# Seven block products in place of eight for half of the batches of a three-layer kernel

## The chip, the cores and the metric

The kernel runs on one core of a Trainium2 chip. Its engines work side by side, each through its own list of instructions in order: TensorE (PE) multiplies matrices into PSUM, VectorE (DVE), ScalarE (ACT) and GpSimd (POOL) work on elements, and SyncE (SP) issues all of the kernel's transfers. GpSimd does not touch PSUM here. They wait for each other by semaphores. The metric is the device time of one execution in microseconds.

## The reference

Four batches of 12 heads go through sigmoid attention; the result, 1792 rows of 768, goes through a gated layer and then through a second one:

```python
scores = scale * np.matmul(q, k.transpose(0, 1, 3, 2)) - np.log(S)
attn_out = np.matmul(1.0 / (1.0 + np.exp(-scores)), v)      # 4 x 12 x 448 x 64
x = attn_out.transpose(0, 2, 1, 3).reshape(B * S, H * D)    # 1792 x 768
xn = x / np.sqrt(np.mean(x * x, axis=-1, keepdims=True) + 1e-06) * rms_g
g = xn @ w_gate                                             # 768 x 1536
x = (g / (1.0 + np.exp(-g)) * (xn @ w_val)) @ w_out         # 1536 x 768
h = x @ w_in                                                # 768 x 2048, "w_in2" below
x = (h - np.tanh(h)) @ w_out2                               # 2048 x 768
```

The weights come as 64-bit floats: each arrives as two 32-bit words and is made a 32-bit float on the chip.

## The kernel before

Activations lie with features on the 128 partitions and the 448 rows of one batch along the free side. All matrices are cut into 128 x 128 blocks; KM = 6, KF1 = 12 and KF2 = 16 blocks make 768, 1536 and 2048. Every operand is split into a high part that TensorE takes exactly and a low rest (`h`, `l`), so one block product is three matmuls of 448 columns, hh, hl and lh, summed in PSUM (`block` in `job_units`, L708 to L715).

**Jobs.** The layers are a list of jobs of six weight blocks (NB = 6): phases Ag (w_gate), Av (w_val), B (w_out), C (w_in2), D (w_out2). A job of Ag, Av or C is one column block m of the weights with all six k; a job of B or D holds blocks of a group of four k (GR = 4) for one or two m, and its sums over the groups are added up in `acc` tiles. Batches 0 and 1 go through all layers together, then batches 2 and 3 (the loop at L297); only the first three m of w_gate and w_val are done for batch 0 and batch 1 apart (`ALONE`). A job for two batches is 36 matmuls. The second half of the list, 68 jobs, is for batches 2 and 3; the attention of these batches runs beside the first half.

**Weights.** For each job `load` brings 768 KB of raw words into one of two `raw` tiles; `conv` makes 32-bit floats of it in a `cv` tile (two of them): `fields` (L365 on ScalarE, L368, L372 or L371, L374), `join` (L378), then `high` (a cast, L274) and `low_part` (a subtraction, L391) into a `whl` tile. Loads are issued four jobs ahead, conversions are made two jobs ahead (`AHEAD`). The second half loads and converts all weights again.

**Ends.** `epilogue` takes a PSUM bank out: sigmoid and two products for the gate, tanh and a difference for w_in2, copy or addition for B and D; `parts` splits the result for the next layer (cast L274, subtraction L649). x of batches 2 and 3 waits in DRAM and comes back near the end of the first half (`reload_x`, `x_chunk`: a product L634, a scaled cast L637, L638).

**Order.** Nothing is issued as written. `add` collects work with the engines that may do it and an assumed time for each; `Plan.issue` goes through it like a clock and places each piece on the engine where it ends first, so the planner chooses between VectorE, ScalarE and GpSimd, and between buffers. TensorE's matmuls of the layers are one stream in the order of the jobs. Many tiles share pools of slots: `unit` (87 tiles of 448 columns), `ps` (the eight PSUM banks). The kernel's own helper `copy` stands at L274, so casts and copies of all kinds have that line.

## Time and profile before

| | us |
|---|---|
| median of 3 runs | 1213.77 |
| the three runs | 1217.71, 1213.77, 1204.66 |
| profiled execution | 1205.45 |
| its span | 1203.7 |

| engine | busy us of the span | share |
|---|---|---|
| TensorE, matmuls | 1171.0 | 97% |
| VectorE | 1011.6 | 84% |
| ScalarE | 558.5 | 46% |
| GpSimd | 213.0 | 18% |

Transfers moved 136.32 MB. The span is what the profiler saw of the profiled execution; 1.75 us of its time lie around it. A matmul's busy time includes its way through the pipeline, so a busy TensorE tells that it did not pause, not how dense its matmuls stand; for that one counts matmuls in a stretch. In rows, L12 is line 12 of the kernel, `out<-in` are the tiles written and read (their numbers left out), x is a count.

### The profile page before, as it was taken

To read this page: it belongs to the slowest core of one execution; us is meant where nothing else is said; L and a number is where in the kernel's file an instruction comes from. 1 tells how busy PE (TensorE), PEld (TensorE's weight loads), DVE (VectorE), ACT (ScalarE), POOL (GpSimd) and SP (SyncE) were. 2 spreads that over 40 slices of the span, in tenths; PEclk is the share of its full clock that TensorE was granted. 3 is DMA by queue.
4 is the path that set the end of the run, shared out by engine and by line. 5 is a ranking of instruction groups with operands and counts; after the bars stand their busy time and mean duration, and the time that the engine had idled before them with its cause. 6 is when DMAs were issued, how large, how long until landed. Compare 5 with 4: busy or idle time off the path is not lost.

```text
span 1203.7 us, 15461 instructions
## 1 busy us (share of the span) xinstructions
PE 1171.0 (97%) x5886; PEld 1027.0 (85%) x5886; DVE 1011.6 (84%) x1429; ACT 558.5 (46%) x858; POOL 213.0 (18%) x131
## 2 busy tenths in 40 slices
...
GB/s 170 191 156 175 67 31 109 135 99 122 106 117 116 68 85 90 117 116 110 113 135 157 98 152 125 111 124 113 105 121 109 62 110 135 121 106 107 110 47 92
DMA packets 41786, 136.32 MB, mean 113 GB/s; under 512 B 7280, under 2 KB 22768, under 8 KB 41712
## 3 DMA queue, kind: packets, MB, share of 16 engines
...
q14 instruction: 28, 0.23, 0.1%
HBM read 127.06 MB, written 8.26 MB: 112 GB/s over the span
## 4 chain that ended last, share of the span: by engine, by line
PE 77%; DVE 12%; ACT 4%; DMA 3%; issue 2%; SPq 1%; POOL 1%; DVEq 0%; ACTq 0%; POOLq 0%
PE ps L712 71%; PE ps L466 3%; DVE raw L374 2%; DVE cv L378 2%; DVE raw L372 1%; PE ps L505 1%; ACT raw L371 1%; DVE unit L649 1%; DMA raw<-in_w_out 1%; DVE cv L368 1%; ACT unit L274 1%; PE ps L559 1%; PE ps L560 1%; SPq L413 1%; DVE unit L274 1%
## 5 line engine op out<-in xcount | busy, mean ns | idle before, releaser
L712 PE MATMUL ps<-unit,whl 128*128 128x448 f32 x4680 | 968.9, 368 | 7.5 <-DVE unit L545 4.5
L712 PEld LDWEIGHTS ps<-unit,whl 128*128 128x128 f32 x4680 | 881.6, 189 | 88.3 <-issue 6.3
L391 POOL TENSOR_TENSOR whl<-cv,whl 128x768 fp32r<-128x768 f32 x84 | 161.2, 1919 | 710.1 <-DVE whl L274 349.1
L365 ACT ACTIVATE cv<-raw 128x768 uint16<-128x768 uint16 x136 | 148.7, 1093 | 195.5 <-POOL whl L391 78.2
L374 DVE TENSOR_SCALAR raw<-raw 128x768 uint16<-128x768 uint16 x136 | 149.1, 1096 | 32.8 <-ACT raw L371 29.7
L378 DVE SCALAR_TENSOR_TENSOR cv<-raw,cv 128x768 uint32<-128x768 uint32 x136 | 139.5, 1026 | 8.3
L649 DVE TENSOR_TENSOR unit<-unit 128x448 fp32r<-128x448 f32 x130 | 100.4, 788 | 20.9 <-ACT unit L274 17.1
L274 ACT CAST unit<-unit 128x448 fp32r<-128x448 f32 (+1 forms) x117 | 64.2, 566 | 105.5 <-DVE unit L662 54.8
L368 DVE TENSOR_SCALAR cv<-raw 128x768 uint16<-128x768 uint16 x136 | 87.7, 645 | 29.5 <-POOL whl L391 25.7
L372 DVE TENSOR_SCALAR raw<-raw 128x768 uint16<-128x768 uint16 x104 | 109.6, 1054 | 3.4
L274 ACT CAST whl<-cv 128x768 fp32r<-128x768 f32 x65 | 54.4, 837 | 110.8 <-PE ps L712 95.3
L676 DVE TENSOR_TENSOR unit<-ps,unit 128x448 f32<-128x448 f32 x120 | 70.1, 618 | 23.2 <-PE ps L712 22.9
L466 PE MATMUL ps<-unit 64*128 64x448 f32 (+1 forms) x576 | 73.6, 388 | 4.7 <-DVE unit L274 2.7
L466 PEld LDWEIGHTS ps<-unit 64*128 64x128 f32 (+1 forms) x576 | 49.1, 176 | 27.6 <-issue 11.3
L545 DVE TENSOR_TENSOR unit<-ps,unit 128x448 fp32r<-128x448 f32 (+1 forms) x96 | 57.6, 619 | 12.4 <-ACT unit L274 10.8
L371 ACT ACTIVATE raw<-raw 128x768 bf16<-128x768 bf16 x32 | 62.0, 1945 | 8.7 <-DVE cv L368 8.6
L666 ACT ACTIVATE unit<-ps 128x448 f32<-128x448 f32 x64 | 31.5, 541 | 63.8 <-PE ps L712 63.8
L476 ACT ACTIVATE ps<-ps 128x448 f32<-128x448 f32 (+1 forms) x96 | 49.4, 533 | 17.7 <-PE ps L466 17.5
L712 PE MATMUL ps<-unit 128*128 128x448 f32 x216 | 51.1, 387 | 0.9 <-ACT unit L476 0.6
L274 DVE CAST unit<-unit 128x448 fp32r<-128x448 f32 (+1 forms) x68 | 35.9, 528 | 16.1 <-DMA unit<-in_qkt 14.4
L712 PEld LDWEIGHTS ps<-unit 128*128 128x128 f32 x216 | 40.6, 194 | 10.1 <-issue 4.2
L476 ACT ACTIVATE unit<-ps 128x448 f32<-128x448 f32 (+1 forms) x96 | 45.7, 542 | 4.1 <-PE ps L466 3.3
...
## 6 DMA issues: line engine op xcount, KB each, us to landing
raw<-in_w_out SPq DMA_DIRECT2D x56, 768.0 KB, 4.3
raw<-in_w_in SPq DMA_DIRECT2D x32, 768.0 KB, 4.3
raw<-in_w_gate SPq DMA_DIRECT2D x24, 768.0 KB, 4.3
raw<-in_w_val SPq DMA_DIRECT2D x24, 768.0 KB, 4.4
...
out<-unit SPq DMA_DIRECT2D x24, 224.0 KB, 2.0
...
```

The lines of the kernel that those rows point to most:

```text
L274: add(engines, lambda e: (nc.scalar.copy if e == "ACT" else nc.vector.tensor_copy)(to(), of()), reads, writes)
L365: add(act(NW), lambda e: nc.scalar.activation(c16(0), low(), AF.Copy, scale=2.0 ** -13, bias=-0.49995), [r["l"]], [c["l"]])
L368: add(dve(NW, fast=True), lambda e: nc.vector.tensor_scalar(out=c16(1), in0=top(), scalar1=0x8000, scalar2=None, op0=ALU.bitwise_and), [r[ ...
L371: add({**dve(NW, fast=True), **act(NW)}, lambda e: nc.scalar.activation(top(BF16), top(BF16), AF.Abs) if e == "ACT" else nc.vector.tensor_ ...
L372: top(BF16), top(BF16), AF.Abs) if e == "ACT" else nc.vector.tensor_scalar(
L374: add(dve(NW, fast=True), lambda e: nc.vector.tensor_scalar(out=top(), in0=top(), scalar1=0x47EF, scalar2=0x3800, op0=ALU.min, op1=ALU.sub ...
L378: add(dve(NW, psum=False), lambda e: nc.vector.scalar_tensor_tensor(out=c.tile, in0=r.tile[:, :, 1], scalar=3, in1=c.tile, op0=ALU.logical ...
L391: add({**dve(wide, psum=False), **pool(wide)}, lambda e, q=q: ENG[e].tensor_sub(ap(q, "l"), f32(q), ap(q, "h").bitcast(F32)), [c["l"], c[" ...
L466: nc.tensor.matmul(ps[i, c].tile[:n, :S], lhsT=f[w].tile[rows, c * P:c * P + n], rhs=f[q].tile[rows, :], start=(w, q) == ("kh", "qh"), sto ...
L476: add(act(S, psum=True), lambda e: nc.scalar.activation(to.tile[at:at + n, :S], ps.tile[:n, :S], AF.Sigmoid, bias=-math.log(S), scale=1.0 ...
L649: add({**pool(S), **dve(S, psum=False)}, lambda e: ENG[e].tensor_sub(c["l"].tile, t.tile, c["h"].tile.bitcast(F32)), [t["t"], kh], [kl])
L712: nc.tensor.matmul(ps.tile[:, :S], lhsT=wt, rhs=a[p].tile, start=first and i == 0, stop=last and i == 2,)
```

## The change

For batches 2 and 3 the layers of w_gate, w_val and w_in2 take two column blocks at a time. The two batches and the two column blocks are rows and columns of a 2 x 2 product of block matrices, the six k being two interleaved sets of three: the left side is A11, A12, A21, A22 (column block m, k set e), the right side B11, B12, B21, B22 (k set e, batch). Seven products of sums take the place of eight: S1 to S4 are sums of left blocks (`sums` in `halves`), T1 to T4 of right blocks (`right_units`), each side is split into high and low afterwards, and the results are put together by seven additions out of PSUM (`plus` in `seven_units`, L849). The w_out and w_out2 layers stay as they were.

Weights of the second half are no longer loaded and converted anew: in the first half each conversion also stores its result in DRAM (`put`: 384 KB from `cv` for w_gate, w_val and w_in2, 768 KB, split already, from the `whl` tile for the others), and `fetch` reads it three jobs ahead (BACK = 3). Raw, split, fetched tiles and the left operands (`op`) share one pool `wt` of 7 slots, where 2 + 4 were; `unit` has 83 slots, not 87. The sums of the left side are in `cv` tiles.

```diff
-N_UNIT, N_MOE, N_RAW, N_WHL = 87, 44, 2, 4
+N_UNIT, N_MOE, N_RAW, N_WT = 83, 44, 2, 7
+N_AGAIN = 3
+BACK = 3
+BATCHES = ((0, 1), (2, 3))
...
-        "raw": (N_RAW, {"raw": N_RAW}),
+        "wt": (N_WT, {"raw": N_RAW, "whl": N_WT - N_RAW, "again": N_AGAIN, "op": N_WT - N_AGAIN}),
...
+    for names, ph, n in (
+        ([(ph, p) for p in range(KF1 // 2) for ph in ("Ag", "Av")], "B", KF1 // GR),
+        ([("C", p) for p in range(KF2 // 2)], "D", KF2 // GR),
+    ):
+        per, at = len(names) // n, 0
+        for g in range(n):
+            to = min((g + 1) * per + 1, len(names))
+            firsts(names[at:to])
+            second(ph, bs, g)
+            at = to
...
+    def fetch(i):
...
+        w = whls[i] = slot("again", wt_p, [P, 2, NW], dt, "wt")
+        add({"SP": (2200, False)}, lambda e: nc.sync.dma_start(out=w.tile if ph in PAIRS else w.tile.bitcast(F32), in_=d.tile),
+            [d[x] for x in "hl"], [w["h"], w["l"]], after=2000)
...
+        def both(to, x, y, sub=True):
+            (o, ok), (a, ak), (b, bk) = of[to], of[x], of[y]
+            add({**dve(NH, psum=False), **pool(NH)}, lambda e: (ENG[e].tensor_sub if sub else ENG[e].tensor_add)(
+                o(), a(), b()), [*ak, *bk], ok)
+
+        def split(*names):
+            t = slot("op", wt_p, [P, 2, 2, NH], F32R, "wt")
+            for n, name in enumerate(names):
...
+                copy({**act(NH), **dve(NH, fast=True)}, hi, a, ak, [t[n, 0]])
+                add({**dve(NH, psum=False), **pool(NH)}, lambda e, a=a, hi=hi, lo=lo: ENG[e].tensor_sub(
+                    lo(), a(), hi().bitcast(F32)), [*ak, t[n, 0]], [t[n, 1]])
...
+            both("S1", "A21", "A22", sub=False)
+            both("S2", "S1", "A11")
+            both("S3", "A11", "A21")
+            both("S4", "A12", "S2")
+
+        return [sums, lambda: split("A11", "S1"), lambda: split("S2", "S3"), lambda: split("A12", "A22"), lambda: split("S4")]
...
+        def put():
+
+            if ph in PAIRS:
+                add({"SP": (1100, False)}, lambda e: nc.sync.dma_start(out=d.tile[:, at % 2], in_=c.tile.bitcast(F32)),
+                    [c["l"], c["h"]], [d["hl"[at % 2]]], after=2000)
+            else:
+                add({"SP": (2200, False)}, lambda e: nc.sync.dma_start(out=d.tile, in_=w.tile.bitcast(F32)),
+                    [w["h"], w["l"]], [d["h"], d["l"]], after=2000)
+
+        if ph in PAIRS:
+            return [fields, lambda: (join(), put()), high, low_part]
+        return [fields, join, high, lambda: (low_part(), put())]
...
+            f["T1"] = right_sum(b12, b11)
+            f["T2"] = right_sum(b22, f["T1"])
+            f["T3"] = right_sum(b22, b12)
+            f["T4"] = right_sum(b21, f["T2"])
...
+    PRODUCTS = {1: ("A11", "B11"), 5: ("S1", "T1"), 6: ("S2", "T2"), 7: ("S3", "T3"),
+                2: ("A12", "B21"), 4: ("A22", "T4"), 3: ("S4", "B22")}
...
+            add(dve(S), lambda e: nc.vector.tensor_add(t.tile, banks[n].tile[:, :S], x.tile), [banks[n]["t"], x["t"]], [t["t"]])
...
+            def run(e):
+                for q, (a, b) in enumerate(("hh", "hl", "lh")):
+                    nc.tensor.matmul(
+                        ps.tile[:, :S], lhsT=part(a), rhs=x[b].tile,
+                        start=i == 0 and q == 0, stop=i == 2 and q == 2)
...
+        if (ph, p) == ("C", 0):
+
+            order = [(n, i) for n in (1, 5, 6, 7) for i in range(2)] + [(n, 2) for n in (1, 5, 6, 7)]
+        else:
+            order = [(n, i) for n in (1, 5, 6, 7) for i in range(3)]
+        order += [(n, i) for n in (2, 4, 3) for i in range(3)]
...
     for j in range(len(jobs)):
+        fetch(j + BACK)
```

How the order moves is shown at three places. First TensorE, from the norm of batch 3 (the four matmuls of 112 x 1) to the end, before:

```order
L712 MATMUL ps<-unit,whl 128x448 x72
L602 MATMUL ps<-ones,unit 112x1 x4
L712 MATMUL ps<-unit,whl 128x448 x18
L612 MATMUL ps<-dg,ones 128x112 x4
L712 MATMUL ps<-unit,whl 128x448 x2682
```

and of the change (L877 are the products, L921 the jobs as before):

```order
L921 MATMUL ps<-unit,wt 128x448 x72
L691 MATMUL ps<-ones,unit 112x1 x4
L921 MATMUL ps<-unit,wt 128x448 x18
L701 MATMUL ps<-dg,ones 128x112 x4
L921 MATMUL ps<-unit,wt 128x448 x234
L877 MATMUL ps<-unit,wt 128x448 x315
L921 MATMUL ps<-unit,wt 128x448 x144
L877 MATMUL ps<-unit,wt 128x448 x252
L921 MATMUL ps<-unit,wt 128x448 x144
L877 MATMUL ps<-unit,wt 128x448 x189
L921 MATMUL ps<-unit,wt 128x448 x144
```

Of the 2682 matmuls in a row 234 end the first half as before; behind them product stretches of 5, 4 and 3 pairs alternate with 144 matmuls of w_out, and behind the rows shown 189, 126, 126 and 63 matmuls of w_in2's products alternate with 144 of w_out2 in the same way.

Second VectorE, early in the gate and value jobs of the second half, before:

```order
L659 TENSOR_TENSOR unit<-ps,unit 128x448 x2
L378 SCALAR_TENSOR_TENSOR cv<-raw,cv 128x768
L274 CAST whl<-cv 128x768
L391 TENSOR_TENSOR whl<-cv,whl 128x768
L368 TENSOR_SCALAR cv<-raw 128x768
L372 TENSOR_SCALAR raw<-raw 128x768
L374 TENSOR_SCALAR raw<-raw 128x768
```

and of the change in the first product stretch:

```order
L849 TENSOR_TENSOR unit<-ps,unit 128x448 x2
L391 TENSOR_TENSOR wt<-cv,wt 128x384
L828 TENSOR_TENSOR unit<-unit 128x448
L381 TENSOR_TENSOR cv<-wt 128x384
L381 TENSOR_TENSOR cv<-wt,cv 128x384
L828 TENSOR_TENSOR unit<-unit 128x448
L276 CAST wt<-cv 128x384
L391 TENSOR_TENSOR wt<-wt 128x384
```

The passes over 768 raw columns are gone; sums (L381) and splits (L276, L391) of left blocks, PSUM additions (L849) and the gate's product in SBUF (L828) stand in their place.

Third SP's transfers in the first half, where w_in2 and w_out2 jobs alternate, before:

```order
L328 DMA raw<-in_w_out 128x1536
L413 DMA unit<-in_qkt 64x448
L328 DMA raw<-in_w_out 128x1536
L423 DMA v<-in_vt 128x256
L328 DMA raw<-in_w_in 128x1536 x3
L423 DMA v<-in_vt 128x256
```

and of the change (L475 and L478 are the stores, L351 the raw loads):

```order
L351 DMA wt<-in_w_out 128x1536
L478 DMA wD_4454<-wt 128x1536
L502 DMA unit<-in_qkt 64x448 x4
L351 DMA wt<-in_w_out 128x1536
L512 DMA v<-in_vt 128x256
L680 DMA x_0_4549<-unit 128x448
L478 DMA wD_4558<-wt 128x1536
L351 DMA wt<-in_w_in 128x1536
```

A store now stands between loads, and a load is issued only when the store ahead of it has what it waits for.

## Rows read from the trace of the kernel before

**Rows 1.** The page, first part: busy time and share of each engine.
```profile
PE 1171.0 (97%) x5886; PEld 1027.0 (85%) x5886; DVE 1011.6 (84%) x1429; ACT 558.5 (46%) x858; POOL 213.0 (18%) x131
```

**Rows 2.** Stretches: length, busy time and count by engine, clock, transfers.
```profile
core 0: us, PE busy (x) PEld busy (x) DVE busy (x) ACT busy (x) POOL busy (x), PEclk, DMA share, GB/s
...
420.00:550.00 130.00, 125.40 (x626) 111.11 (x625) 119.77 (x170) 73.30 (x119) 27.55 (x18) 0.98 0.32 106
...
670.00:680.00 10.00, 7.14 (x27) 5.58 (x26) 9.79 (x13) 3.48 (x7) 5.53 (x4) 0.85 0.23 79
...
702.00:1150.00 448.00, 448.00 (x2213) 415.13 (x2211) 388.97 (x511) 165.16 (x211) 81.02 (x43) 1.00 0.33 113
```

**Rows 3.** The chain that ended last, in order of time: start, length, what.
```profile
645.21 0.69 PE ps L602 x8
...
676.26 523.36 PE ps L712 x2572
```

**Rows 4.** Timeline of TensorE: one-batch jobs, then two-batch jobs.
```profile
135.69 15.08 PE L712 MATMUL ps<-unit 128*128 128x448 f32 x72
...
630.46 14.75 PE L712 MATMUL ps<-unit,whl 128*128 128x448 f32 x72
```

**Rows 5.** Groups by line from 702 to 1150 us: busy us, mean ns, idle before.
```profile
L372 DVE TENSOR_SCALAR raw<-raw 128x768 uint16<-128x768 uint16 x51 | 53.5, 1048 | 1.7
L649 DVE TENSOR_TENSOR unit<-unit 128x448 fp32r<-128x448 f32 x61 | 45.9, 768 | 11.7 <-ACT unit L274 9.8
...
L676 DVE TENSOR_TENSOR unit<-ps,unit 128x448 f32<-128x448 f32 x50 | 29.4, 621 | 1.5 <-PE ps L712 1.4
...
L391 POOL TENSOR_TENSOR whl<-cv,whl 128x768 fp32r<-128x768 f32 x42 | 81.5, 1941 | 388.8 <-DVE whl L274 194.6 <-ACT whl L274 130.1 <-DVE unit L676 64.1
```

**Rows 6.** Instructions of lines 649 and 391: duration ns min/median/max.
```profile
L649 DVE TENSOR_TENSOR unit<-unit x130: 601/626/2206, 97.3 to 1173.6; 128x448 fp32r<-128x448 f32 x130
L649 POOL TENSOR_TENSOR unit<-unit x6: 1148/1158/1167, 263.6 to 968.9; 128x448 fp32r<-128x448 f32 x6
...
L391 POOL TENSOR_TENSOR whl<-cv,whl x84: 1799/1852/2429, 167.8 to 1171.4; 128x768 fp32r<-128x768 f32 x84
L391 DVE TENSOR_TENSOR whl<-cv,whl x46: 937/958/983, 90.7 to 1142.2; 128x768 fp32r<-128x768 f32 x46
L391 DVE TENSOR_TENSOR unit<-cv,unit x12: 548/551/558, 33.7 to 82.4; 128x384 fp32r<-128x384 f32 x12
```

**Rows 7.** Groups by line, whole execution: casts of 384 columns on VectorE.
```profile
L274 DVE CAST unit<-cv 128x384 fp32r<-128x384 f32 x7 | 2.3, 357 | 0.3
```

**Rows 8.** Timeline at 1061 us: start, length, engine, line.
```profile
1061.70 1.15 DVE L667 TENSOR_TENSOR unit<-ps,unit 128x448 f32<-128x448 f32 x2
1061.93 1.85 POOL L391 TENSOR_TENSOR whl<-cv,whl 128x768 fp32r<-128x768 f32 x1 [5.44 <-DVE whl L274]
...
1062.96 1.84 DVE L649 TENSOR_TENSOR unit<-unit 128x448 fp32r<-128x448 f32 x2
```

**Rows 9.** Timelines of GpSimd, VectorE and TensorE around 670 us.
```profile
664.32 11.21 POOL L634 TENSOR_TENSOR unit<-unit 128x448 f32<-128x448 f32 x7
...
667.85 1.84 DVE L372 TENSOR_SCALAR raw<-raw 128x768 uint16<-128x768 uint16 x1
...
675.73 14.58 PE L712 MATMUL ps<-unit,whl 128*128 128x448 f32 x60 [2.80 <-ACT unit L274]
```

**Rows 10.** Transfers by issue: count, KB each, us from issue to landing.
```profile
raw<-in_w_out SPq DMA_DIRECT2D x56, 768.0 KB, 4.3
...
out<-unit SPq DMA_DIRECT2D x24, 224.0 KB, 2.0
```

**Rows 11.** Waits, whole execution: us in total, times, longest us.
```profile
ACT cv L365 <- POOL whl L391: 78.2, 46, 5.1
...
ACT cv L365 <- DMA raw<-in_w_out: 18.0, 7, 4.4
...
SPq L328 <- DVE cv L378: 754.7, 124, 19.5
```

191 lines of the change are left out of this document (151 added, 40 removed).

## The prediction

> **What bounds the kernel now.** I read the busy shares first. TensorE is busy 1171.0 of 1203.7 us, VectorE 1011.6, and no other engine is over half [rows 1]. A busy TensorE need not be a dense one, so I read stretches next: from 702 to 1150 us, all inside the half for batches 2 and 3, TensorE never pauses, its clock is granted in full, and 2213 matmuls take 448 us, 202.4 ns each; VectorE is busy 388.97 of those 448 us (87%) beside it [rows 2]. The chain of waits says the same: it ends in one piece of 2572 matmuls from 676.26 us on [rows 3]. So a matmul fewer in this half is worth 202.4 ns, as long as VectorE keeps up. The first half is different: from 420 to 550 us VectorE is busy 119.77 of 130 us and TensorE pauses for 4.6 us, and from 670 to 680 it pauses again, its granted clock at 0.85 of full in the mean, so in part at the lower of its two levels [rows 2]. There VectorE is the engine that a little more work would show on.
>
> **What goes away.** A pair of column blocks took 2 x 6 x 2 blocks of 3 matmuls, 72; now it takes seven products of 3 blocks of 3 matmuls, 63. There are 6 + 6 + 8 = 20 pairs, so 180 matmuls go: 2448 become 2268, and the order's rows on TensorE sum to that. At 202.4 ns this is **-36.4 us**. One thing could spoil the price: a product sends its nine matmuls into one PSUM bank, where the old block went to and fro between two. The one-batch jobs at the start also write one bank in a row: 72 matmuls took 15.08 us, and 72 two-batch ones 14.75 [rows 4]. Spread evenly that is 4.6 ns each, on 1260 product matmuls 5.8 us; as it may as well be one pause of 0.33 us at the start of the stretch, I charge nothing and keep 5.8 us for the range.
>
> Also gone are the 68 conversions of raw weights in this half, each with three or four passes of VectorE over 768 columns, one of them at 1048 ns [rows 5]. In their place VectorE gets, from the first product on, 35 PSUM additions for the first five pairs (0.618 us as the 621 ns of L676 [rows 5]), seven for each later pair, and SBUF work on 384 columns (0.551 us) and 448 columns (0.626 us) [rows 6]. Counted from the order and priced so (casts of 384 columns 0.357 [rows 7]), VectorE has 59.4 us of work in the first stretch of 315 product matmuls, which takes TensorE 63.8 us; 43.9 against 51.0 in the next; 32.2 against 38.3; in w_in2 34.8 against 38.3, 21.9 against 25.5 twice, 10.2 against 12.8. The output layers between them need 144 matmuls, 29.1 us, and only some 12 us of VectorE. On paper it fits.
>
> **GpSimd is what may break the fit.** It gets about 100 instructions in this half: 44 of 448 columns (1.158 us [rows 6]) and 55 of 384 (half of the 1.852 us for 768, so an estimate of 0.93), 104 us or 5.2 us a pair. While GpSimd runs, VectorE's SBUF work is slowed: at 1061.93 a GpSimd subtraction of 1.85 us starts, the two PSUM operations beside it keep their pace, but the two SBUF ones behind them take 1.84 us [rows 8] where two are worth 1.25 [rows 6]. That is 0.59 us lost. Taken over 702 to 1150 the loss of L649 is 61 x (768 - 626) ns = 8.7 us for 81.5 us of GpSimd, 0.11 [rows 5, 6]; in the burst at 664 us, where seven GpSimd operations follow each other for 11.21 us, an operation worth 1.048 us takes 1.84, a loss of 0.43 of the time [rows 5, 9]. With 0.25 between these, the first stretch needs 59.4 + 6.5 = 65.9 us of VectorE against 63.8, 2.1 us too much, and w_in2's first stretch 0.4; with half, the excess sums to 8.6 + 3.3 + 1.7 + 4.3 + 1.6 + 1.6 = 21 us. I take **+6 us**, nearer the low end: VectorE also waits in order now and then, but the next pair's operands are made ahead, an eighth bank is spare, and at 87% it cost TensorE nothing before [rows 2]. The Trainium skill (SBUF — State Buffer, "Who interferes with whom") states a harder rule: GpSimd and VectorE hold a shared port pair in turn, and the loser is blocked for the whole instruction. By that rule the loss depends on what VectorE has beside GpSimd, nothing for a PSUM addition and the whole rest of the instruction for SBUF work; the pair of PSUM operations and the pair of SBUF ones in [rows 8] agree with it, and the sum by it would lie at the high end, 15 us above mine.
>
> **The change of halves.** Between the sums for batch 3's norm and the first product, TensorE has 234 matmuls, 47.4 us. VectorE has 88 instructions there, 53.6 us by the prices above: the last conversion, the scaled x, sums and splits of the right-hand blocks, the first pair's left-hand blocks. Ten GpSimd operations stand beside it (10 us, in a burst, so 5 us more). VectorE would be 11 us late. The first product needs only A11 and B11, so some of that is hidden by the first pair's own 12.8 us; and the old kernel pauses 2.80 us at this place too [rows 9]. Between -2.8 and +11 I take **+6 us**.
>
> **Output layer to w_in2.** The right-hand sums for the last third wait for the last addition of w_out. 24 matmuls (4.9 us) of the first two thirds run meanwhile; behind the last matmul stand two additions and up to six SBUF operations, 1.24 + 3.8 = 5.0 us plus the casts. Between 0 and +5: **+2 us**.
>
> **First half.** Each of the 68 conversions now also stores its weights: 384 KB from cv for gate, value and w_in2, 768 KB from the split tile for the rest. The trace has no such store; 224 KB stored land after 2.0 us and 768 KB loaded after 4.3 [rows 10], so 384 KB lie between, by size near 2.7. It holds cv, of which there are two, while cast and subtraction read it anyway (1.9 us when GpSimd subtracts); ScalarE already waits 78.2 us for that release [rows 11], without TensorE stopping often. On SP's queue a store waits for join or subtraction, and the next weight load stands behind it; loads already wait there 754.7 us, almost all for the same join [rows 11]. So I charge the store itself nothing. But the new order gives VectorE nine more subtractions (0.958 us [rows 6]) and seven more casts before the norm of batch 3, which stands at 645.21 us [rows 3]: at most 15 us in 645; 130 of these 645 us are the stretch where the chain runs through VectorE, so **+3 us**, with 0 below and, should loads or cv come late, tens of us above (a rival). Fetches replace loads of equal size in the second half and are issued three jobs, some 30 us, ahead: nothing.
>
> **Sum.** -36.4 + 6 + 6 + 2 + 3 = -19.4. The profiled execution took 1205.45 us, so 1186.0 by its scale. It lies 8.3 us under the median of the three runs, whose spread is 1204.66 to 1217.71; a median of the changed kernel should lie half of that higher, so I say **1190 us**.
>
> **Rivals.**
> Clean gain: VectorE keeps pace everywhere and only the matmuls count: 1205.45 - 36.4 = 1169, or 1173 on my scale. For it: no pause from 702 to 1150 at 87% [rows 2]. Against it: the change of halves already pauses [rows 9]. 0.17.
> VectorE and GpSimd become the bound in the product stretches: the 21 us in place of 6: 1201, or 1205. For it: the burst in [rows 9]; against it: PSUM additions are a third to a half of VectorE's time there, and those keep their pace beside GpSimd [rows 8]. 0.2, and no change that can be told. The rule of the Trainium skill named above (SBUF — State Buffer) would make this the likelier case.
> The stores delay the conversions of the first half: 34 two-batch jobs of gate, value and w_in2 hold cv until a store has landed, and the store waits its turn behind loads on SP. If a job ends 2 us later than TensorE's cover, 34 x 2 = 68 us, so 1183 + 68 = 1251. It decides from about 1 us a job on (35 us). For it: VectorE at 92% from 420 on and 18.0 us in which ScalarE waits for late loads of w_out already [rows 11]; against it: conversions are made two jobs ahead. 0.11, and slower.
> That the products are not saved is excluded: TensorE's order holds 2268.
>
> **Numbers.** My forecast itself has 0.52, with 1180 to 1201 as its own range. About 1% is what a measurement of this kernel can tell from none. Faster by over 1%: 0.17 plus most of 0.52, 0.62. Within 1%: the slow end of my case and the second rival, 0.27. Slower: 0.11. The range of 8 in 10 goes from the clean gain less the old pause (1170) to the second rival with the dearer bank price (1211).
>
> **What would show it.** Right: one run of 2268 matmuls near 202 ns with VectorE's share under 95% in product stretches; the first half ending near 645 to 650 us at the norm of batch 3. Wrong: matmuls of L877 at 207 ns or more; pauses of TensorE before L877 released by VectorE's splits (L391) or by PSUM additions (L849) over 10 us in all; ScalarE's L443 or VectorE's first field waiting for stores from cv; the norm of batch 3 later than 660 us.

## The result and the profile after

| | before | changed |
|---|---|---|
| median, us | 1209.22 (4 runs) | 1171.48 (4 runs) |
| runs from to, us | 1204.14 to 1217.71 | 1169.76 to 1172.57 |
| ratio of the times | | 0.968, 95% interval 0.9613 to 0.9747 |
| profiled execution, us | 1205.45 | 1172.02 |
| its span, us | 1203.7 | 1170.2 |
| TensorE busy, us (share) | 1171.0 (97%) | 1137.1 (97%) |
| VectorE busy, us (share) | 1011.6 (84%) | 922.5 (79%) |
| bytes moved, MB | 136.32 | 158.35 |

The kernel became faster, as forecast, and its time lies inside the range (1170 to 1211). But the forecast change was -19.4 us on the profiled execution, and -33.4 us came: costs that the sum had charged were not there, and the first half became shorter, where it had been expected to grow.

The busy shares of the changed kernel's page, the answer to [rows 1]:

```profile
PE 1137.1 (97%) x5706; PEld 989.6 (85%) x5706; DVE 922.5 (79%) x1487; ACT 489.4 (42%) x866; POOL 211.5 (18%) x169
```

180 matmuls went (5886 to 5706). The timeline of the changed kernel's TensorE, the answer to [rows 3] and [rows 9]; columns: start us, us, engine, line, operation, tiles, count, and in brackets the idle time before and who ended it. L691 and L701 are the two sums of a norm, L877 a product, L921 a block of the other layers:

```profile
383.51 1.15 PE L701 MATMUL ps<-dg,ones 112*128 112x112 f32 x8 [2.68 <-DVE dg L696]
384.42 6.32 PE L921 MATMUL ps<-unit,wt 128*128 128x448 f32 x30
...
497.63 3.02 PE L921 MATMUL ps<-unit,wt 128*128 128x448 f32 x12 [1.11 <-DVE unit L276]
...
539.42 3.02 PE L921 MATMUL ps<-unit,wt 128*128 128x448 f32 x12 [0.97 <-DVE unit L634]
...
635.89 0.85 PE L691 MATMUL ps<-ones,unit 128*112 128x1 f32 x8
...
644.00 1.15 PE L701 MATMUL ps<-dg,ones 112*128 112x112 f32 x8 [3.43 <-DVE dg L696]
...
695.76 65.26 PE L877 MATMUL ps<-unit,wt 128*128 128x448 f32 x315
760.86 29.92 PE L921 MATMUL ps<-unit,wt 128*128 128x448 f32 x144
...
916.22 27.07 PE L921 MATMUL ps<-unit,wt 128*128 128x448 f32 x131 [1.85 <-DVE unit L276]
...
949.66 3.92 PE L877 MATMUL ps<-unit,wt 128*128 128x448 f32 x18 [1.30 <-DVE unit L738]
954.41 29.86 PE L877 MATMUL ps<-unit,wt 128*128 128x448 f32 x146 [0.84 <-DVE unit L738]
984.11 29.35 PE L921 MATMUL ps<-unit,wt 128*128 128x448 f32 x144
...
1139.31 27.07 PE L921 MATMUL ps<-unit,wt 128*128 128x448 f32 x131 [1.02 <-DVE unit L276]
```

Cut at the norm of batch 3 and at the start of the second half, the span of 1203.7 us became 1170.2 as follows. In the kernel before the second cut is found by counting: 2448 matmuls before the last one, at 703.52 us.

| | before | changed | difference | forecast |
|---|---|---|---|---|
| to the norm of batch 3 | 645.05 | 635.89 | -9.16 | +3 |
| from there to the second half | 58.47 | 59.87 | +1.40 | +6 |
| from there to the end | 500.14 | 474.48 | -25.66 | -36.4 + 6 + 2 = -28.4 |

So the second half came out near its sum, though not by its terms, and the first half is where the forecast failed most. Stretches of the changed kernel, the answer to [rows 2]: length, busy time and count by engine, granted clock, transfers:

```profile
696.00:761.00 65.00, 65.00 (x316) 59.05 (x315) 56.89 (x109) 18.66 (x36) 13.42 (x12) 1.00 0.28 93
...
791.00:843.00 52.00, 52.00 (x253) 47.23 (x253) 42.19 (x78) 16.49 (x33) 12.29 (x12) 1.00 0.28 92
...
872.00:912.00 40.00, 40.00 (x195) 36.32 (x195) 30.13 (x55) 10.45 (x21) 9.42 (x9) 1.00 0.29 99
```

These are the first three product stretches: TensorE never stops in them, and VectorE is busy 88, 81 and 75% of the time. The new transfers, the answer to [rows 10] (KB each, us from issue to landing):

```profile
wD<-wt SPq DMA_DIRECT2D x16, 768.0 KB, 3.4
wt<-wD SPq DMA_DIRECT2D x16, 768.0 KB, 4.3
...
wC<-cv SPq DMA_DIRECT2D x16, 384.0 KB, 2.6
...
wAg<-cv SPq DMA_DIRECT2D x12, 384.0 KB, 2.9
```

A store of 384 KB lands after 2.6 to 2.9 us (estimated: near 2.7), and a fetch takes as long as the load of equal size did. Of SP's waits for the join, 754.7 us before [rows 11], only 297.7 lay ahead of 640 us; the rest went with the raw loads of the second half. What is left, for a store (L475) and for a load (L351):

```profile
SPq L475 <- DVE cv L456: 143.5, 29, 11.5
...
SPq L351 <- DVE cv L456: 73.0, 12, 17.4
```

### The profile page after: what moved, and what is told of

The parts are those of the page before. It is cut to its first block, busy times and chain, and to the rows that moved or that the text cites. A ratio compares the mean times of both kernels' runs of the same rounds, so it can differ in the third digit from the quotient of the medians.

```text
span 1170.2 us, 15352 instructions
## 1 busy us (share of the span) xinstructions
PE 1137.1 (97%) x5706; PEld 989.6 (85%) x5706; DVE 922.5 (79%) x1487; ACT 489.4 (42%) x866; POOL 211.5 (18%) x169
## 2 busy tenths in 40 slices
DMA packets 48699, 158.35 MB, mean 135 GB/s; under 512 B 8048, under 2 KB 23536, under 8 KB 48624
## 5 line engine op out<-in xcount | busy, mean ns | idle before, releaser
L921 PE MATMUL ps<-unit,wt 128*128 128x448 f32 x3240 | 676.4, 368 | 5.4 <-DVE unit L276 4.0
L921 PEld LDWEIGHTS ps<-unit,wt 128*128 128x128 f32 x3240 | 607.2, 188 | 67.1 <-issue 5.9
L877 PE MATMUL ps<-unit,wt 128*128 128x448 f32 x1260 | 260.1, 367 | 2.1 <-DVE unit L738 2.1
L877 PEld LDWEIGHTS ps<-unit,wt 128*128 128x128 f32 x1260 | 236.4, 188 | 24.6 <-DVE unit L738 2.9
L803 DVE TENSOR_TENSOR unit<-ps,unit 128x448 f32<-128x448 f32 x120 | 69.3, 618 | 67.8 <-PE ps L921 67.7
L276 ACT CAST unit<-unit 128x448 fp32r<-128x448 f32 (+1 forms) x141 | 75.9, 565 | 108.6 <-DVE unit L803 25.1
L469 POOL TENSOR_TENSOR wt<-cv,wt 128x768 fp32r<-128x768 f32 x30 | 56.4, 1879 | 294.9 <-DVE wt L276 118.0
L443 ACT ACTIVATE cv<-wt 128x768 uint16<-128x768 uint16 x68 | 74.4, 1095 | 77.4 <-POOL wt L469 39.3
L276 ACT COPY unit<-ps 128x448 f32<-128x448 f32 (+1 forms) x73 | 39.1, 537 | 149.7 <-PE ps L877 80.8
L849 DVE TENSOR_TENSOR unit<-ps,unit 128x448 f32<-128x448 f32 x140 | 81.6, 618 | 14.3 <-PE ps L877 13.3
L276 ACT CAST wt<-cv 128x384 fp32r<-128x384 f32 (+1 forms) x84 | 50.4, 613 | 96.4 <-PE ps L877 37.2
L452 DVE TENSOR_SCALAR wt<-wt 128x768 uint16<-128x768 uint16 x68 | 73.5, 1081 | 13.2 <-ACT wt L449 11.4
L776 DVE TENSOR_TENSOR unit<-unit 128x448 fp32r<-128x448 f32 x106 | 74.2, 709 | 7.3 <-ACT unit L276 4.9
L456 DVE SCALAR_TENSOR_TENSOR cv<-wt,cv 128x768 uint32<-128x768 uint32 x68 | 65.8, 968 | 3.6
L450 DVE TENSOR_SCALAR wt<-wt 128x768 uint16<-128x768 uint16 x52 | 55.9, 1075 | 1.6
L446 DVE TENSOR_SCALAR cv<-wt 128x768 uint16<-128x768 uint16 x68 | 45.8, 676 | 13.8 <-POOL wt L469 8.6
L921 PE MATMUL ps<-unit 128*128 128x448 f32 x216 | 51.5, 388 | 2.8 <-ACT unit L565 1.9
L921 PEld LDWEIGHTS ps<-unit 128*128 128x128 f32 x216 | 40.6, 194 | 12.4 <-issue 4.2
```

The source lines that it names most:

```text
L276: add(engines, lambda e: (nc.scalar.copy if e == "ACT" else nc.vector.tensor_copy)(to(), of()), reads, writes)
L443: add(act(NW), lambda e: nc.scalar.activation(c16(0), low(), AF.Copy, scale=2.0 ** -13, bias=-0.49995), [r["l"]], [c["l"]])
L452: add(dve(NW, fast=True), lambda e: nc.vector.tensor_scalar(out=top(), in0=top(), scalar1=0x47EF, scalar2=0x3800, op0=ALU.min, op1=ALU.sub ...
L456: add(dve(NW, psum=False), lambda e: nc.vector.scalar_tensor_tensor(out=c.tile, in0=r.tile[:, :, 1], scalar=3, in1=c.tile, op0=ALU.logical ...
L469: add({**dve(wide, psum=False), **pool(wide)}, lambda e, q=q: ENG[e].tensor_sub(ap(q, "l"), f32(q), ap(q, "h").bitcast(F32)), [c["l"], c[" ...
L776: add({**pool(S), **dve(S, psum=False)}, lambda e: ENG[e].tensor_sub(c["l"].tile, t.tile, c["h"].tile.bitcast(F32)), [t["t"], kh], [kl])
```

## The experiments

The norm of batch 3 is a good mark: up to it the kernel before and the changed one give TensorE the same work. Where it stands in each profile, one execution each (TensorE's first sum, us; e7_early, which moves this norm itself, is left out):

| kernel | us | kernel | us |
|---|---|---|---|
| before | 645.1 | changed | 635.9 |
| before, again (before_2) | 647.7 | changed, again (after_2) | 639.1 |
| before, 85 tiles (f3_before85) | 646.0 | 82 tiles (f2_unit82) | 640.2 |
| before, 83 tiles (p1_unit83) | 641.4 | three raw tiles (f1_raw3) | 634.6 |
| shared pool (e1_shared) | 638.6 | no GpSimd later (e6_nopool) | 634.8 |
| five split tiles (e2_whl5) | 638.5 | extra matmuls later (e5_aside) | 638.7 |
| three raw tiles (e2_raw3) | 636.6 | products alone (e9_products) | 638.4 |
| stores alone (e3_stores) | 630.9 | scratch alone (e8_scratch) | 641.9 |
| before, matmuls in the norms (g1_fill) | 643.8 | changed, matmuls in the norms (g2_fill) | 639.6 |

**Parts of the change in the first half.** Four kernels take over single parts of the change or something near them: the pool shared by raw and split weights; a fifth split tile, which the shared pool allows; a third raw tile, which the change does not have; and the stores of all converted weights, which nothing reads back. The first three also have 83 tiles of 448 columns, as the change has; the fourth keeps 87. The cuts below leave out lines (`...`).

```diff
e1_shared:
-N_UNIT, N_MOE, N_RAW, N_WHL = 87, 44, 2, 4
+N_UNIT, N_MOE, N_RAW, N_WT = 83, 44, 2, 7
...
+        "wt": (N_WT, {"raw": N_RAW, "whl": N_WT - N_RAW}),
...
e2_whl5:
+N_UNIT, N_MOE, N_RAW, N_WHL = 83, 44, 2, 5
e2_raw3:
+N_UNIT, N_MOE, N_RAW, N_WHL = 83, 44, 3, 4
e3_stores:
...
-        return [fields, join, high, low_part]
...
+        if ph in ("Ag", "Av", "C"):
+            return [fields, lambda: (join(), put()), high, low_part]
+        return [fields, join, high, lambda: (low_part(), put())]
```

> The kernel before with one part of the change alone: raw and split weight tiles share one pool of 7 slots (2 + 4 apart before), unit has 83 slots. No stores, no products. Theory A (the first half of the changed kernel is 9 us ahead at the norm of batch 3 because a raw load now takes a slot that has long been free, and no longer waits for the join of two jobs before): norm of batch 3 at 634 to 638 us (645.21 before), total about 1196, SP's waits for the join far under 754.7 us. Theory B (the 9 us are scatter between executions, or come from the planner's other choices in the rest of the change): norm at 643 to 648, total as before. After the norm both expect the old 558 us.

> The kernel before with pools apart, but five split weight tiles instead of four (unit 83 slots): the same memory as the shared pool. Theory A (which slot the raw load takes decides): norm of batch 3 still at 643 to 648 us, total within 3 us of before. Rival C (one split tile more is what helps, sharing is not needed): norm at 634 to 638, total about 1196.

> The kernel before with pools apart, but three raw tiles instead of two (four split tiles, unit 83 slots): a load then waits for the join of three jobs before instead of two. Theory A (late raw loads are what stops TensorE in the first half): norm of batch 3 at 634 to 639 us, total about 1196, ScalarE's waits for raw loads (18.0 us for w_out alone) mostly gone. Theory B or C: norm at 643 to 648, total as before.

> The kernel before, pools as before, plus the stores of all 68 weight conversions of the first half to DRAM (nothing reads them back; the second half loads and converts as before). This is the price of the stores by themselves. The prediction's sum charges nothing: norm of batch 3 at 645 to 648 us, total 1204 to 1209. The prediction's rival (stores hold cv and stand before loads on SP): 1 us and more for each of 34 jobs, norm at 680 us or later, total 1240 and more.

Measured beside the kernel before (median 1206.73 of 31 runs): e1_shared 1210.88, ratio 1.0017 (0.9981 to 1.0053); e2_whl5 1203.86, 0.9958 (0.9914 to 1.0003); e2_raw3 1199.55, 0.9947 (0.9905 to 0.9989); e3_stores 1196.29, 0.9917 (0.9881 to 0.9952). No cost of the stores shows; the kernel with stores alone is even the one that comes to the norm earliest. The rival of delayed conversions falls. No part has the -9.2 us to itself: each of the four has the norm 6.5 to 14.1 us before the 645.1 us of the kernel before. Not all of this is seen in the times: for e1_shared about 1196 us was expected, and the lowest of its ten runs is 1204.51, where the kernel before has 1202.58 beside it. Its profile takes 570.6 us behind the norm, where the kernel before takes 558.6; the matmuls' pace, below, makes most of the difference.

**Is it scatter?** The kernel before once more, and with 83 tiles alone:

```diff
p1_unit83:
-N_UNIT, N_MOE, N_RAW, N_WHL = 87, 44, 2, 4
+N_UNIT, N_MOE, N_RAW, N_WHL = 83, 44, 2, 4
```

> The kernel before, unchanged, profiled a second time. Two questions. First, how much of the 9 us by which the changed kernel stands ahead at the norm of batch 3 is scatter of the kernel before: theory B (scatter) expects the norm several us off 645 us, theory D (the order of the kernel before has stops of its own in the first half, which any new plan loses) expects 643 to 647. Second, the pace: theory P says TensorE's stream runs at 202.7 or at 206.7 ns per matmul, set anew at each stop and kept until the next, so a total near 1204 us goes with 202.7 ns behind the last stop and a total near 1214 us with 206.7.

> The kernel before with the unit pool cut from 87 to 83 slots and nothing else: a new plan without any of the change's parts. Theory D (the 6 to 14 us that all variants so far gain at the norm come from losing the old order's stops, whatever the edit): norm at 634 to 642 us. Rival: slots of weights or stores are what helps: norm at 643 to 648 us. The fastest runs 1195 to 1200 by theory D, 1203 to 1206 by the rival; by theory P a second group some 10 us higher in either case.

before_2 took 1207.93 us; p1_unit83 1211.38, ratio 0.9988 (0.9948 to 1.0027), and its norm is 3.7 us earlier than in the first profile of before, hardly more than the 2.7 us between the two executions of before. The norm of before_2, 647.7 us, lies just past the 643 to 647 expected. In before_2 TensorE stops at the same places with the same lengths as in the first profile of before: 3.80, 2.10, 1.76 and 0.52 us, where that has 3.75, 1.98, 2.03 and 0.53. So the stops belong to the kernel and its order of work, not to the execution. Timeline of TensorE in before_2:

```profile
388.41 1.15 PE L612 MATMUL ps<-dg,ones 112*128 112x112 f32 x8 [3.80 <-DVE dg L607]
389.32 6.87 PE L712 MATMUL ps<-unit,whl 128*128 128x448 f32 x25
...
505.10 4.58 PE L712 MATMUL ps<-unit,whl 128*128 128x448 f32 x12 [2.10 <-DVE unit L545]
...
549.33 0.48 PE L712 MATMUL ps<-unit,whl 128*128 128x448 f32 x1 [1.76 <-DVE unit L545]
550.33 3.97 PE L712 MATMUL ps<-unit,whl 128*128 128x448 f32 x11 [0.52 <-DVE unit L545]
```

The same three places in the changed kernel are the first rows of its timeline above: stops of 2.68, 1.11 and 0.97 us. And what follows is as telling as the stop: twelve matmuls take 4.58 us behind the 2.10 us stop and 3.02 behind the 1.11 us one. The granted clock, last but two in a row, says why. Stretches behind the second and the third stop in before_2:

```profile
505.20:508.20 3.00, 2.94 (x8) 2.40 (x9) 3.00 (x7) 1.75 (x4) 0.00 (x0) 0.59 0.38 158
549.40:552.40 3.00, 2.48 (x7) 1.97 (x8) 2.97 (x6) 0.66 (x1) 1.82 (x1) 0.62 0.76 256
```

and in the changed kernel:

```profile
497.70:500.70 3.00, 2.94 (x14) 2.48 (x15) 2.96 (x6) 1.57 (x3) 0.00 (x0) 1.00 0.60 237
539.50:542.50 3.00, 2.94 (x14) 2.48 (x15) 2.93 (x6) 1.12 (x2) 1.30 (x1) 1.00 0.92 324
```

Behind these longer stops TensorE mostly has its lower level of 1.2 GHz for a while (0.59 and 0.62 in the mean), behind the shorter ones 2.4. Such a stop is paid twice. Against before_2 the three places give 1.1 + 1.0 + 1.3 us of stops and some 1.6 + 1.6 + 1.4 us of matmuls at the lower level, 8 us in all; against the first profile of before likewise 8 of the 9.2. That little else counts can be seen by matching the 3170 matmuls ahead of the norm one by one: the changed kernel leads the first profile of before by 1.1 us at 380 us, 3.8 at 400 and still at 495, 6.2 at 520 and 540, 9.2 at 560 and at the norm. The 1.1 us at 380 arose ahead of 200 us, where the two profiles of before differ by 2 us themselves. The second execution of the changed kernel (after_2) gains less at these places, 6.5 us: behind its first stop the clock fell too.

**The clock's part alone.** The two executions of the changed kernel have the same order and the same first stop, 2.68 and 2.70 us. In the first (its rows are above) the matmuls of the norm and the 30 behind them take 7.2 us, in after_2 8.8:

```profile
385.13 1.96 PE L701 MATMUL ps<-dg,ones 112*128 112x112 f32 x8 [2.70 <-DVE dg L696]
386.77 7.20 PE L921 MATMUL ps<-unit,wt 128*128 128x448 f32 x30
```

The granted clock behind the stop, in the first and in after_2:

```profile
384.50:387.50 3.00, 3.00 (x17) 2.79 (x16) 2.83 (x7) 2.00 (x3) 0.00 (x0) 1.00 0.04 16
```

```profile
386.00:389.00 3.00, 3.00 (x13) 2.80 (x12) 2.83 (x7) 2.08 (x3) 0.00 (x0) 0.56 0.10 41
```

So the clock alone was worth 1.6 us here. Two further runs try to hold it: eleven small extra matmuls, no part of the result, keep TensorE at work while it waits for `dg` in the norms of batches 2 and 3.

```diff
g1_fill (kernel before), g2_fill (changed kernel), in norm(b):
+        if b > 1:
+            add({"PE": (3000, False)}, lambda e: [nc.tensor.matmul(
+                ps2.tile[:, :P], lhsT=ones, rhs=ones, start=True, stop=True) for _ in range(11)], [ms["t"]], [ps2["t"]], stream="norm")
         add({"PE": (1500, False)}, rows, [dg["t"]], [ps2["t"]], stream="norm")
```

> The kernel before with eleven extra 128x128 matmuls (no part of the result) on TensorE just ahead of the matmuls that wait for dg in the norms of batches 2 and 3; that wait stays. Theory C (a long stop costs a second time, by a lower granted clock behind it): the extra matmuls fill 2 to 3 of the 3.75 us at 385 us, the end of the wait stays where it is, and the 30 matmuls behind it take 6.1 to 6.5 us in place of 7.89 at a granted clock near 1.00, so the kernel is 1.5 us further on behind the norm of batch 2. Rival: the clock behind the stop is low whatever TensorE did in it, or the 30 matmuls are slow for another reason, 7.9 us again. The total moves by less than the runs scatter (1202 to 1215 us).

> The same in the changed kernel. Theory C: the 110 matmuls behind the norm of batch 3 (24.09 to 24.49 us, 219 to 223 ns each) come at 203 to 207 ns, 22.4 to 22.9 us, so the first product stands some 1.6 us earlier behind that norm; 1167 to 1173 us. Rival: they stay at 24 us or more, the matmuls there being slow because VectorE hands over operands late; 1170 to 1176 us.

The norm of batch 2 in the kernel before, then in g1_fill:

```profile
385.72 1.15 PE L612 MATMUL ps<-dg,ones 112*128 112x112 f32 x8 [3.75 <-DVE dg L607]
386.63 7.89 PE L712 MATMUL ps<-unit,whl 128*128 128x448 f32 x30
```

```profile
382.28 2.62 PE L622 MATMUL ps<-ones 128*128 128x128 f32 x22
385.91 1.15 PE L612 MATMUL ps<-dg,ones 112*128 112x112 f32 x8 [1.01 <-DVE dg L607]
386.82 5.13 PE L715 MATMUL ps<-unit,whl 128*128 128x448 f32 x24
```

The 24 matmuls behind the stop take 214 ns each; the 30 at this place in the kernel before took 7.89 us, 263 ns each. The granted clock behind the stop, before and in g1_fill:

```profile
386.70:389.70 3.00, 3.00 (x11) 2.71 (x10) 2.30 (x6) 1.82 (x3) 0.00 (x0) 0.53 0.00 0
```

```profile
386.70:389.70 3.00, 3.00 (x18) 2.79 (x17) 1.50 (x3) 1.37 (x2) 0.33 (x1) 1.00 0.39 162
```

The extra matmuls move other work too: 6 of the layers' matmuls stand between the norm's sums and its second product where 12 stood (18 in the norm of batch 3), and from the sums to the end of the wait 5.66 us pass, 7.15 before; in the norm of batch 3 of g2_fill 5.0, and 8.1 in the changed kernel. So these two runs show that the clock stays up where TensorE has work in the stop and at most 1.01 us of it is left idle, not what that alone saves. Time 1210.78 us, ratio 0.9966 (0.9927 to 1.0005): some 1.5 us are too little to be told from the runs' scatter. In the changed kernel the 3 us behind the norm of batch 3, with and without the extra matmuls:

```profile
644.90:647.90 3.00, 3.00 (x12) 2.64 (x11) 2.83 (x4) 0.53 (x1) 0.00 (x0) 0.54 0.17 66
```

```profile
645.60:648.60 3.00, 3.00 (x17) 2.75 (x17) 2.83 (x4) 0.54 (x1) 0.00 (x0) 1.00 0.14 53
```

From the norm to the first product (at 697.40 us) g2_fill needs 57.8 us, the changed kernel 59.9 and, in after_2, 58.9; 1170.66 us, ratio 0.9661 (0.9606 to 0.9715), no different from the changed kernel's. The 122 matmuls behind the norm took 213 ns each, not the 203 to 207 expected: part of their slowness has another cause, which is left open.

A long stop does not always bring the clock down. In g1_fill the next stop, 2.64 us at 503 us, has 1.00 behind it, as have 1.88 us in e2_raw3 and 1.81 in e2_whl5, while 2.14 us in f3_before85 and 2.00 in after_2 have 0.54 and 0.50.

**Does any new order do it?** The number of tiles alone, in either kernel, and three raw tiles in the changed one:

```diff
f3_before85:
-N_UNIT, N_MOE, N_RAW, N_WHL = 87, 44, 2, 4
+N_UNIT, N_MOE, N_RAW, N_WHL = 85, 44, 2, 4
f2_unit82:
-N_UNIT, N_MOE, N_RAW, N_WT = 83, 44, 2, 7
+N_UNIT, N_MOE, N_RAW, N_WT = 82, 44, 2, 7
f1_raw3:
-N_UNIT, N_MOE, N_RAW, N_WT = 83, 44, 2, 7
+N_UNIT, N_MOE, N_RAW, N_WT = 83, 44, 3, 7
```

> The kernel before with 85 tiles of 448 columns in place of 87, nothing else; no instruction is added or removed, and TensorE's order is the same. Theory O (stops of the first half are accidents of the order): TensorE's stops near 385, 502 and 547 us change in size, and the norm of batch 3 comes 2 to 9 us before the 645.2 and 647.9 us of the kernel before, as with 83 tiles (3.7 earlier). Rival E (the changed kernel's own edits make the gain): the norm within 1.5 us of 645.2 to 647.9 and the stops as before.

> The changed kernel with 82 tiles of 448 columns in place of 83, nothing else. Theory O: the norm of batch 3 moves by 2 us or more from 635.9 and 639.1, either way, because the side work is ordered anew; total 1166 to 1180 us. Rival E: the norm within 1.5 us of these two and the total within 2 us of 1172.

> The changed kernel with three of its seven weight tiles for raw weights and four for split ones, in place of two and five. If loads of raw weights still held the first half, it gains as the kernel before did with three raw tiles (norm of batch 3 8.5 us earlier): 1162 to 1168 us. Theory: the changed kernel has few of those waits left (VectorE's conversions stand ahead of the loads for 73 us in place of 755), so only the order moves: norm within 4 us of 635.9 to 639.1, 1167 to 1178 us; with one split tile fewer the products' operands may come later, which would show as stops before the first products.

Beside the kernel before (1207.6, 13 runs): f3_before85 1206.15, ratio 0.9965 (0.9928 to 1.0002); f2_unit82 1173.57, 0.974 (0.9709 to 0.9772); f1_raw3 1169.52, 0.9719 (0.9693 to 0.9744). With 85 tiles the stops stayed: 3.78, 2.14 and 2.13 us. That was a miss: not any new order loses them. It is a mild test, though: by line and kind of tile 28 of VectorE's 816 instructions ahead of the norm stand elsewhere, and 70 with 83 tiles. With 82 tiles the second stop of the changed kernel went and the third grew to 2.65 us, yet norm and time stayed as rival E had them. In the changed kernel's family the norm stays between 634.6 and 640.2 us; with the order of before, or nearly so (before, before_2, f3_before85, g1_fill), between 643.8 and 647.7. So the gain does belong to what the change rearranges, but 83 tiles alone bring 3.7 us, with them the shared pool 6.5 and a third raw tile 8.5, and stores alone 14.1, and they don't add up. Which part shortens which stop is left open. The time of f1_raw3 can't be told from the changed kernel's.

**The second half: scratch without products, products without scratch.** e8_scratch keeps eight products and reads split weights back; e9_products has the seven products and loads and converts the weights anew.

```diff
e8_scratch (against e1_shared):
...
+        if again(i):
+            return [lambda: None] * 4
...
+        fetch(j + 3)
e9_products (against the changed kernel):
...
-        fetch(j + BACK)
...
+                add({"SP": (2200, False)}, lambda e, r=r, m=m: nc.sync.dma_start(out=r.tile, in_=PAIRS[ph][0][2 * at + m]), reads, [r["l"], r["h"]], after=2000)
```

> The scratch alone: shared pool of 7 slots, the split weights of the two-batch jobs are stored to DRAM in the first half and read back for batches 2 and 3, eight products as before (the six one-batch column blocks of gate and value are loaded and converted anew). VectorE loses some 60 conversions of the second half. If TensorE's count of matmuls sets the second half, as the prediction says, nothing is gained behind the norm: 556 to 562 us from norm to end at 202.7 ns, 566 to 572 at 206.7; norm 631 to 640; fastest runs 1190 to 1198. Rival: the conversions did cost TensorE something in the second half (waits the chain does not show): under 550 us from norm to end.

> The seven products alone: the raw weights of batches 2 and 3 are loaded and converted anew as before, into four cv tiles, six slots in the shared pool, nothing stored or read back. VectorE then has some 3.7 us of conversion for each of 68 column blocks on top of the 337 us counted for the products: about 590 us for 459 us of matmuls. Expected by the prediction's way of summing (VectorE sets the pace once its work exceeds TensorE's): second half some 100 us or more longer than the changed kernel's, total 1260 to 1320 us, so slower than before. Rival (waits and engines overlap well enough, ScalarE and GpSimd take the excess): total under 1200.

e8_scratch: 1215.3 us, ratio 1.0014 (0.997 to 1.0058), the lowest of its ten runs 1206.41; its norm at 641.9 us and its fastest runs missed the 631 to 640 and 1190 to 1198 us expected. e9_products: 1311.1 us, in one run. Stretch from 702 to 1150 us of e8_scratch:

```profile
702.00:1150.00 448.00, 448.00 (x2169) 406.87 (x2168) 144.62 (x249) 49.70 (x93) 1.16 (x1) 1.00 0.32 107
```

VectorE's 388.97 us of [rows 2] are down to 144.62 and nothing is gained, since TensorE was the limit there and stays it. In e9_products the load on VectorE turns the other way:

```profile
700.00:1150.00 450.00, 365.59 (x1631) 323.09 (x1630) 408.12 (x645) 198.75 (x297) 55.76 (x47) 0.91 0.26 89
```

VectorE is at 91% and TensorE idle for 84 of 450 us, with four `cv` tiles and six slots of weights, so with other buffers than the changed kernel. The scratch by itself is worth nothing; it is what lets the products pay.

**VectorE's margin in the product stretches.** All of GpSimd's sums, splits and products of the second half go to VectorE:

```diff
e6_nopool (one place of six):
-            add({**dve(NH, psum=False), **pool(NH)}, lambda e: (ENG[e].tensor_sub if sub else ENG[e].tensor_add)(
+            add(dve(NH, psum=False), lambda e: (ENG[e].tensor_sub if sub else ENG[e].tensor_add)(
```

> The changed kernel with the second half's sums, splits and products of activations taken from GpSimd and given to VectorE (the weights' block splits too), nothing else moved. Theory M (VectorE has margin in the product stretches: 56.9 busy of 65.0 us in the first, 42.2 of 52, 30.1 of 40): some 7 us of subtractions move to VectorE in each of the first stretches, 64 of 65 us in the first, so TensorE stops little from 696 us on, under 5 us more than in the changed kernel; the change of halves, already at 54.5 of 60 us, takes most of the loss; 1174 to 1186 us. The prediction's rival (the product stretches are at VectorE's limit): stops before the products released by VectorE of 15 us or more from 696 us on, 1190 us or more. If GpSimd's slowing of VectorE was worth more than its help: 1172 us or less.

1179.06 us, ratio 0.9733 (0.9675 to 0.9791); the changed kernel beside it 1172.5. Its stops from the first product on sum to 12.2 us, the changed kernel's to 5.0, so 7 more: a little over the 5 that margin allowed, far from the 15 of the rival. Its change of halves, where most of the loss had been expected, took 57.8 us, less than the changed kernel's: a miss. Of the 12.2 us, 5.2 lie inside product stretches, where the changed kernel has none; the stop behind the third of them grew from 1.85 to 3.56. Timeline of TensorE and the first stretch:

```profile
732.98 2.09 PE L877 MATMUL ps<-unit,wt 128*128 128x448 f32 x9 [1.95 <-DVE unit L849]
...
738.86 22.15 PE L877 MATMUL ps<-unit,wt 128*128 128x448 f32 x108 [1.44 <-ACT unit L276]
```

```profile
692.60:761.00 68.40, 64.72 (x317) 59.05 (x316) 64.17 (x127) 14.28 (x28) 0.00 (x0) 1.00 0.29 95
```

With VectorE at 94% the stops come that the prediction had feared; at the changed kernel's 88% there are none.

**The pace of the matmuls, and the change of halves.** In the changed kernel 315 products take 65.26 us, 206.7 ns each from start to start, but 126 at 1013 us 25.70, 202.7 each (a row's length also holds the way of its last matmul through the pipeline). Three runs ask whether this belongs to the stage, and whether earlier side work would help the change of halves: the changed kernel again, with four extra small matmuls at each switch of layers, and with the side work ahead of the halves a job earlier.

```diff
e5_aside:
...
+        if j >= half and (j == half or (jobs[j][4] is None) != (jobs[j - 1][4] is None)):
+            aside()
e7_early:
-        (last_c - 4, last_c - 2, norm_units(3, 0)),
-        (last_c, half, again()),
+        (last_c - 5, last_c - 3, norm_units(3, 0)),
+        (last_c - 2, half, again()),
```

> The changed kernel again, as the mark for the three runs beside it. Theory O (the order sets the stops): the same stops of TensorE at the same places as in the first profile of the changed kernel (2.7 us before the norm of batch 2, about 3.4 us before the norm of batch 3, 1.9 us at 916), the norm of batch 3 within 2 us of 635.9; 1168 to 1175 us. If the first half's gain was scatter between executions, the norm of batch 3 lies elsewhere, between 632 and 648.

> The changed kernel with four small extra matmuls (128x128, no part of the result) on TensorE at the start of the second half and at each of the 13 switches between product stretches and output-layer stretches. Theory P (the matmuls of a stretch run at one of two paces, 202.7 or 206.7 ns, set anew where something else interrupts them and held till the next interruption): in place of one slow piece from 696 to 916 us, single stretches are slow and others fast, and the pace changes at the extra matmuls only; 14 x 4 extra matmuls cost about 4 us, so 1166 to 1176 us. Rival S (the pace belongs to the stage, gate, value and w_out operands being slow ones): all stretches from 696 to 916 at 206.7 as before, all later ones at 202.7, and the extra matmuls add their 4 us: 1174 to 1178 us.

> The changed kernel with the first half's side work a job earlier: attention of batch 3 ends one job earlier, its norm one job earlier, and the making of the right-hand blocks starts two jobs earlier. Theory O (the order of the work beside the matmuls sets the stops of the first half and of the change of halves): the 3.4 us stop at the norm of batch 3 and the slow stretch behind it (3.9 us lost from the norm to the first product) go or shrink, but attention packed into fewer jobs can add stops before 600 us; 1164 to 1174 us. Rival: VectorE's whole work before the first product sets that point whatever the order: the first product at 694 to 698 us as before.

Beside the kernel before (1213.73, 7 runs): after_2 1172.5, ratio 0.9675 (0.9619 to 0.9731); e5_aside 1179.81, 0.9731 (0.9672 to 0.9791); e7_early 1176.79, 0.9702 (0.963 to 0.9773). after_2 was expected to have its norm within 2 us of 635.9; it is 3.2 us later, with the stops at the same places. Timeline of TensorE in after_2:

```profile
697.99 64.00 PE L877 MATMUL ps<-unit,wt 128*128 128x448 f32 x315
761.83 29.34 PE L921 MATMUL ps<-unit,wt 128*128 128x448 f32 x144
...
914.38 28.34 PE L921 MATMUL ps<-unit,wt 128*128 128x448 f32 x131 [2.00 <-DVE unit L276]
```

The same 315 products of the same stage, at 202.7 ns. So the pace isn't the stage's, and that rival falls; nor is it VectorE's doing, since e8_scratch has 2169 matmuls in its 448 us, 206.5 ns each, with VectorE busy a third of the time and the clock at 1.00. e5_aside ran at 202.7 from the first product on almost throughout, so it doesn't show where the pace changes; its extra matmuls took 0.81 us at each of 14 places, 11 us and not the 4 that I had reckoned. That is more than its whole loss of 7.3 us, since the stops beside them shrank (1.11 us at the first, 2.00 in after_2). e7_early took 2.8 us more than the 1174 expected at most. In it the stop at the norm of batch 3 shrank to 1.25 us, but one of 3.96 came at 668 us, and the first product stands at 697.1 us, between the 695.8 and 698.0 of the changed kernel's profiles: moving the work earlier only moved the stop. What sets the pace is left open.

## Why the prediction was half right

Its main term, the matmuls saved, came as forecast; the step that failed is the charge for the first half, and with it most of the smaller charges were too high. The number of the rival "clean gain", 1173, is nearest to the 1171.48 measured, but that is luck: it left the first half as it was and had -36.4 us in the second, where -9.16 and -25.66 came.

- **180 matmuls at 202.4 ns, -36.4 us: right.** In after_2, where the pace is 202.7 ns all through, the second half takes 471.7 us, 28.4 less than the 500.1 before. 180 x 202.7 ns is 36.5 us. Its four stops give back 8.1: 5.1 are the idle time of the rows, 1.3 are matmuls at the lower clock behind the first of them (131 in 28.34 us, where the changed kernel's first profile has 27.07), and 1.7 are what the row of a stop doesn't show, since its idle time begins when the last matmul has gone through the pipeline, and since the first matmuls behind it take some 305 to 355 ns each. From start to start of matmuls the stops cost 3.8 us at 914, 2.7 at the two before products and 1.6 at 1139. The price of a single bank didn't show: 126 products take 25.70 us and 144 two-batch matmuls 29.35, both 202.7 ns each from start to start.
- **Product stretches, +6 us: mis-sized; 0 us of stops.** The first stretch was counted as 65.9 us of VectorE and has 56.9, GpSimd's slowing included. The share of 0.25 for that slowing was high: in the second half a split (L776) takes 737 ns, and 624 in e6_nopool, where GpSimd rests; such losses over the groups of both come to about 17 us for 101.7 us of GpSimd, 0.17. And GpSimd works 13.42 us in the first stretch, where 5.2 us a pair had made 26. That makes 2.3 us of slowing there in place of 6.5; the other 4.8 us were in the count of VectorE's work, and where is not traced. The rule of the Trainium skill (SBUF — State Buffer, "Who interferes with whom") is borne out in whom it names: PSUM additions take 618 ns with GpSimd and 619 without, subtractions of two SBUF operands lose. In the same section the Trainium skill words the block of a whole instruction for VectorE's 2-port modes, and of two SBUF inputs it says that they contend with a GpSimd instruction that reads SBUF; how much they lose was the prediction's own reading. The losses are small in sum, 2.3 us in the first stretch, and VectorE had the slack to lose them in, so that case, 15 us above mine, did not come about.
- **A pace of 206.7 ns up to 914 us, +4.2 us from the first product on, wasn't in the sum.** It took most of what the +6 had been set aside for. The prediction had 207 ns as a sign that the bank was dearer; after_2 with the same order shows that it isn't that.
- **Output layer to w_in2, +2 us: right.** 1.30 + 0.84 us of idle time, 2.7 from start to start, released by L738, the splits of the right-hand blocks. The stops of 1.85 and 1.02 us just behind product stretches were not foreseen: there `w_out` and `w_out2` wait for a cast (L276) in the epilogue of the products before them; from start to start they cost 2.4 and 1.6 us.
- **Change of halves, +6 us: too high.** +1.4 and, in after_2, +0.5. The old pause of 2.80 us [rows 9] went, and one of 3.43 before `L701` came, with a granted clock of 0.54 behind it. VectorE wasn't 11 us late. Its work was counted about right: 54.49 us in this stretch, 91 instructions, where the sum had 88 and 58.6 us.

```profile
636.00:696.00 60.00, 56.21 (x271) 50.23 (x270) 54.49 (x91) 19.55 (x39) 18.61 (x14) 0.97 0.36 135
```

But the sum set against it the 234 matmuls behind `L701` alone, 47.4 us, and left out the 8.1 us from the norm's sums to `L701`, with 18 matmuls and the stop; VectorE works in those too.

- **First half, +3 us: the step that failed.** I charged VectorE's added work, up to 15 us, by the share of the stretch in which the chain runs through VectorE. But a busier VectorE cost nothing where TensorE was dense, and it was dense nearly everywhere: from 130 to 380 us VectorE went from 208.96 to 214.66 us of 250, and TensorE was busy 249.7 before and after. Before, then changed:

```profile
130.00:380.00 250.00, 249.75 (x1279) 222.49 (x1278) 208.96 (x301) 126.03 (x209) 47.85 (x30) 1.00 0.29 97
```

```profile
130.00:380.00 250.00, 249.74 (x1276) 222.20 (x1275) 214.66 (x319) 127.77 (x206) 34.72 (x22) 1.00 0.47 163
```

What the first half loses is lost at three stops; the changed order shortens them from 3.8, 2.0 and 2.5 to 2.7, 1.1 and 1.0 us, and with the stops the time at the lower clock behind them goes: 8 us, 6.5 in after_2. So -9.2 us came in place of +3. Why the new order shortens them is open. I read the pauses of [rows 2] as VectorE's limit, where they are single late hand-overs.

- **Stores and fetches, nothing: right**, by e3_stores for the stores and by e8_scratch for the fetches, beside which TensorE never stops from 702 to 1150 us.
- **Scale, +4 us: wrong.** The changed kernel's runs lie within 3 us, those of before within 14. Two paces for 2448 matmuls would spread them by 10 us (4 ns x 2448), and e1_shared and e8_scratch, with as many, do run at the slower one; but both profiles of before run at the faster, so that this is what spreads its runs is not shown.

From 1190 to 1171.5 that is -12.2 for the first half, -6 + 4.2 for product stretches and pace, -4.6 for the change of halves, -4.5 for the scale (the median is 0.5 under the profiled time, not 4 over it), and, from start to start, +4.0 for the two unforeseen stops and +0.7 for those before w_in2: 1171.6.
